# Relative-bias attention with a low-rank mixer: column halves of the first weight, an earlier cast, an even spread of the first MLP chunk, and a last output tile in two halves

## The chip, the cores and the metric

The kernel runs on one core of a Trainium2 chip. The metric is the device time of one execution in microseconds (us), as a median of several executions. The profiler's span of the same execution is some 1.8 us shorter, as it begins and ends with recorded work: 408.5 us of span belong to 410.26 us of time. A program on one core has no second die to compare with, so an execution is called fast when it lies within 1.5% of the fastest of its kernel.

## The reference, cut to what matters

```python
# q, k, v: (8 batches, 8 heads, 576 positions, 64), f32
scores = q @ k.T / 8 + bias_table[bucket(|i - j|)]         # relative-position bias
x      = softmax(scores) @ v                               # heads side by side: (8, 576, 512)
h      = (x.transpose(0, 2, 1) @ U @ V).transpose(0, 2, 1) # U, V mix positions, rank 32
u      = x + h
out    = u + relu(u @ w_ch1) @ w_ch2                       # 512 -> 2048 -> 512
```

## The kernel before

The attention runs in 32 **slots**, one for each batch and pair of heads (slots 0 to 3 are batch 0, and so on), and from slot 4 on each slot has three **segments**. The channel MLP runs in **chunks** of 512 positions: chunk 0 is batch 0, and chunk 8 takes the 64 left-over positions of all batches. A chunk has 128 matmuls of 512 columns, 64 with `w1` and 64 with `w2`. They are work that needs no VectorE or ScalarE result of the attention at hand, so they are fed into the segments one by one, to keep TensorE busy while other engines work. The generator below makes a chunk, and `Work.run(us)` issues its matmuls until so many microseconds of them are out.

```python
def chunk(j, tail):
    rhs = uT[j % 3] if j < B else uT_rem
    g = gsb.tile([128, NHT, S0], BF16, name="g")
    for nt in range(NHT):                            # 16 tiles of the hidden 2048
        gp_ = acc()                                  # one of three PSUM accumulators
        for ct in range(4):
            nc.tensor.matmul(gp_, lhsT=w1b[:, ct, nt * 128 : (nt + 1) * 128],
                             rhs=rhs[:, ct, :], start=(ct == 0), stop=(ct == 3))
            yield 0.216
        ...                                          # relu into g, by VectorE or ScalarE
    for tt in range(4):
        op = acc()
        for nt in range(NHT):
            nc.tensor.matmul(op, lhsT=g[:, nt, tt * 128 : (tt + 1) * 128],
                             rhs=w2b[:, nt, :], start=(nt == 0), stop=(nt == NHT - 1))
            yield 0.216
        ob = osb.tile([128, DM], FP32, name="ob")
        ...                                          # VectorE: ob = op + u, then the store(s)
```

Everything that turns f32 in DRAM into bf16 on chip is issued by GpSimd (POOL), in program order. The part that matters is this, with the line that issues the q and k tiles of batch 2 much later:

```python
load_w1(0)                        # w1[0:256, :]  -- rows: all columns of the first two row blocks
load_rem(1, 0); load_rem(1, 1)
qk1 = [[load_pair(which, 0) for which in range(2)]]

def more_loads():
    ...
    load_w1(1)                    # w1[256:512, :]
    ...
    for pr in range(2, NPAIR):
        qk1.append([load_pair(which, pr) for which in range(2)])
    for i in range(2):
        load_w2(i)                # 1 MB each, as bf16
# ... in the second segments of slots 4, 5, 7, 8, 9, 10: five more loads each (batch 2)
```

From slot 4 to slot 10 TensorE also transposes the q and k of the next slot. At slot 7 that is the first slot of batch 2, whose q lies in four tiles, loaded one by one:

```python
def pair_transposes(g, which):
    ...
    for t in range(NT):           # 4 tiles of q or k, and one of left-over rows
        ...
            src = qk2[which][t][:, cols]
        nc.tensor.transpose(tp[:, t * 128 : (t + 1) * 128], src, ident)
    nc.vector.tensor_copy(qkT[b % 2][:, pr, which, :], tp[:, 0:SP])
```

The softmax here doesn't subtract the row's maximum and nothing guards it: scores larger than these inputs give would overflow.

Of the kernel before, what the change touches and what calls it, by code (L numbers as in the profile page):

```python
# [15 lines left out]
ALU = mybir.AluOpType  # L16
# [14 lines left out]
def _ap_with(ap: bass.AP, offset, pattern):  # L31
    return dataclasses.replace(ap, offset=offset, ap=[list(p) for p in pattern])
# [3 lines left out]
def kernel(  # L36
# [12 lines left out]
    nc = tc.nc  # L49
    B, H, S, D = q.shape  # L50
    NB = bias_table.shape[0]
    DM = H * D
    DH = moe_w_ch1.shape[1]
# [7 lines left out]
    S0 = 512  # L61
    P4W = 704
    NPAIR = H // 2
    NHT = DH // 128
# [47 lines left out]
    w1b = const.tile([128, 4, DH], BF16)  # L112
    w2b = const.tile([128, NHT, DM], BF16)
# [225 lines left out]
    def cast_uv():  # L339
        nc.vector.tensor_copy(out=upad[:, 0:4, 0:R], in_=u_st[:, 0:4, :])  # L340
        for par in range(2):
            rows = slice(par * 64, par * 64 + 64)
            nc.vector.tensor_copy(out=upad[rows, 4 + par, 0:R], in_=u_st[rows, 4, :])
        nc.vector.tensor_copy(out=vpad[0:R, 0:S], in_=v_st)

    def load_w1(i):
        nc.gpsimd.dma_start(
            out=w1b[:, 2 * i : 2 * i + 2, :],
            in_=moe_w_ch1[i * 256 : (i + 1) * 256, :].rearrange("(t p) c -> p t c", p=128),
        )  # L350

    def load_w2(i):
# [7 lines left out]
    def acc():  # L360
        return ps_a.tile([128, 512], FP32, name="acc")
# [3 lines left out]
# [4 lines that stand above are left out]
            gp_ = acc()  # L369
            for ct in range(4):  # L370
                nc.tensor.matmul(  # L371
                    gp_,
                    lhsT=w1b[:, ct, nt * 128 : (nt + 1) * 128],
                    rhs=rhs[:, ct, :],
                    start=(ct == 0),
                    stop=(ct == 3),
                )
                yield 0.216
            if (nt % 2) if tail else clock["seg"] > 1.5:
                nc.scalar.activation(g[:, nt, :], gp_, AF.Relu)  # L380
            else:
                nc.vector.tensor_relu(out=g[:, nt, :], in_=gp_)  # L382
        for tt in range(4):
            op = acc()
            for nt in range(NHT):
                nc.tensor.matmul(  # L386
                    op,
                    lhsT=g[:, nt, tt * 128 : (tt + 1) * 128],
                    rhs=w2b[:, nt, :],
                    start=(nt == 0),  # L390
                    stop=(nt == NHT - 1),
                )
                yield 0.216
            ob = osb.tile([128, DM], FP32, name="ob")
            ur = u_tok[j % 3][:, :, tt, :] if j < B else u_rem[tt]
            nc.vector.tensor_tensor(  # L396
                out=ob.rearrange("p (a c) -> p a c", a=NPAIR),
                in0=op.rearrange("p (a c) -> p a c", a=NPAIR),
                in1=ur,
                op=ALU.add,  # L400
            )
            if j < B:
                nc.sync.dma_start(out=out[j, tt * 128 : (tt + 1) * 128, :], in_=ob)
            else:
                for par in range(2):
                    nc.sync.dma_start(
                        out=out[2 * tt + par, S0:S, :],
                        in_=ob[par * 64 : par * 64 + 64, :],
                    )

    ready = [False] * (B + 1)

    class Work:
        def __init__(self):
            self.gens = [(j, chunk(j, j >= B - 1)) for j in range(B + 1)]
            self.at = 0
            self.credit = 0.0

        def run(self, us):
            self.credit = min(self.credit + us, 4.0)  # L420
            while self.credit > 0 and self.at < len(self.gens):
                j, gen = self.gens[self.at]
                if not ready[j]:
                    self.credit = 0.0
                    return
                c = next(gen, None)
                if c is None:
                    self.at += 1
                    continue
                self.credit -= c  # L430
                clock["seg"] += c

        def finish(self):
# [132 lines left out]
    def band(g, kt):  # L566
        pr = g % NPAIR
        if kt < NKT:
            q0 = max(0, 128 * kt - 128)
            q1 = min(S, 128 * kt + 256)  # L570
            d0 = q0 - (128 * kt - 128)
            t = p_sb[g % 2][:, kt, :, q0:q1]
            e = eb[:, 2 * pr : 2 * pr + 2, d0 : d0 + q1 - q0]
        else:
            t = p4_sb[g % 2][:, 384:SP]
            e = eb4[:, pr, :]
        nc.vector.tensor_tensor(out=t, in0=t, in1=e, op=ALU.mult)  # L577
# [39 lines left out]
    def normalise(g, heads=(0, 1)):  # L617
        if g not in x_pr:
            x_pr[g] = xpp.tile([128, NT, 128], BF16, name="xp")
        xo = x_pr[g].rearrange("p t (h d) -> p t h d", h=2)  # L620
        for hh in heads:
            o = o_ps.pop((g, hh))[:, 0 : NT * 66].rearrange("p (t c) -> p t c", c=66)
            rcp = recipp.tile([128, NT], FP32, name="rcp")
            nc.vector.reciprocal(rcp, o[:, :, 64])  # L624
            rbc = _ap_with(rcp, rcp.offset, [rcp.ap[0], [1, NT], [0, 64]])
            nc.vector.tensor_tensor(  # L626
                out=xo[:, :, hh], in0=o[:, :, 0:64], in1=rbc, op=ALU.mult
            )
# [90 lines left out]
    work = Work()  # L719
# [51 lines left out]
    def emit_held(g, seg):  # L771
        now[0] = 3 * g + seg
        n = 0
        while held and (held[0][1] <= g or (held[0][0] <= now[0] and n < 2)):
            held.pop(0)[2]()
            n += 1
# [15 lines left out]
    def main_scores(g, kt):  # L792
        posts = [score(g, kt), score(g, kt + 1)]
        clock["seg"] = 0.0
        for p in posts:
            p()
# [5 lines left out]
    def rem_scores(g):  # L802
        for p in [score(g, 4), score(g, 5)]:
            p()

    def pvs(g, *ks):
        for kt in ks:
            pv(g, kt)

    def bands(g, *ks):  # L810
        for kt in ks:
            band(g, kt)
# [20 lines left out]
    kts(1, 3)  # L833
    pvs(0, 4, 0, 1, 2, 3)
    bands(1, 4, 0)
    normalise(0)
    cast_uv()
    rem_scores(2)
    kts(2, 0)
    first_transposes(3, qk0.pop(3), one)  # L840
# [45 lines left out]
    for g in range(NPAIR, NG):  # L886
        b, pr = divmod(g, NPAIR)
        for seg in range(3):
            emit_held(g, seg)
            box = []  # L890
            if seg:
                main_scores(g, 2 * seg - 2)
            else:
                box = remainder_scores(g)
            if seg == 1:
                n = 0
                if g == NPAIR or g == 2 * NPAIR or (pr == 3 and 1 < b < B - 2):
                    pool_order += load_tasks(b + 1 if pr == 0 else b + 2)
                if g in (4, 5, 7, 8, 9, 10):
                    n = 5  # L900
                elif b > 1:
                    if pr == 3 and b < B - 2 or pr in (0, 2) and b < B - 1:
                        n = 5
                if n:
                    nc.gpsimd.tensor_copy(out=gate, in_=x_pr[g - 1][0:1, 0, 0:2])  # L905
                    for _ in range(n):
                        pool_order.pop(0)()
            work.run(1.7 if g < 2 * NPAIR + 2 else 2.2)
            for p in box:
                p()  # L910
            if g == NPAIR:
                pass
            elif seg == 0:
                if g > NPAIR + 1:
                    mix_h(g - 2)
            elif seg == 2:
                mix_t(g - 1, nc.scalar.copy)
            if seg and NPAIR < g < 2 * NPAIR:
                put_off.pop(0)()
            if seg == 0:  # L920
                if g + 1 < 3 * NPAIR:
                    pair_transposes(g + 1, 0)
                band(g, 4)
                if g > NPAIR:
                    pv_head(g - 1, 0)
            elif seg == 1:
                if g + 1 < 3 * NPAIR:
                    pair_transposes(g + 1, 1)
                band(g, 0)
                band(g, 1)  # L930
                if g > NPAIR:
                    pv_head(g - 1, 1)
                if b > 1 and pr == 1:
                    ready[b - 1] = True
            else:
                band(g, 2)
                band(g, 3)
    assert not pool_order and not held
    g = NG - 1
# [48 lines left out]
```

## Time and profile before

| kernel before | |
|---|---|
| time, median (lowest to highest) | 410.66 us (410.39 to 410.82) |
| span of the profiled execution | 408.5 us |
| TensorE busy | 389.5 us, 95% |
| full stretch of TensorE | 96 to 403.7 us |

The prediction below goes through the page and the timelines. One more view of the kernel before turned out to be the most useful, and I made it only afterwards: the busy time in three stretches that are cut at events of TensorE itself. The columns are the window, its length, the busy time of PE (TensorE), PEld (its weight loads), DVE (VectorE), ACT (ScalarE) and POOL with counts, then granted clock, DMA share and GB/s.

```profile
36.60:39.03 2.43, 1.71 (x16) 0.85 (x14) 0.92 (x3) 1.45 (x3) 1.23 (x2) 1.00 2.18 148
39.03:94.06 55.03, 53.20 (x582) 30.84 (x579) 42.54 (x96) 29.58 (x39) 30.50 (x44) 1.00 1.39 130
94.06:408.50 314.44, 309.26 (x2735) 164.45 (x2733) 173.34 (x367) 147.98 (x207) 67.80 (x96) 1.00 0.76 87
```

I call what lies ahead of the first window **stage A** (start to the first MLP matmul), and the three windows **B** (to the first matmul of slot 4), **C** (to the first matmul of chunk 1) and **D** (to the end). What to see: B, C and D are lengths between two events in one execution, so a late start does not enter them, except where a transfer's landing decides. These views end at the span as the page prints it, rounded to 0.1 us. For D, where differences of 0.07 us matter, the text and the table take the end from the trace's last record (408.49 us here, so D is 314.43).

### The profile page before, as it was taken

To read this page: it belongs to the slowest core of one execution; us is meant where nothing else is said; L and a number is where in the kernel's file an instruction comes from. 1 tells how busy PE (TensorE), PEld (TensorE's weight loads), DVE (VectorE), ACT (ScalarE), POOL (GpSimd) and SP (SyncE) were. 2 spreads that over 40 slices of the span, in tenths; PEclk is the share of its full clock that TensorE was granted. 3 is DMA by queue.
4 is the path that set the end of the run, shared out by engine and by line. 5 is a ranking of instruction groups with operands and counts; after the bars stand their busy time and mean duration, and the time that the engine had idled before them with its cause. 6 is when DMAs were issued, how large, how long until landed. Compare 5 with 4: busy or idle time off the path is not lost.

```text
span 408.5 us, 9084 instructions
## 1 busy us (share of the span) xinstructions
PE 389.5 (95%) x3684; PEld 212.8 (52%) x3684; DVE 246.3 (60%) x558; ACT 205.0 (50%) x284; POOL 125.7 (31%) x179
## 2 busy tenths in 40 slices
PE   3779999999999999999999999999999999999995
PEld 1456555555555555555555555555555554444442
DVE  6886897667765667557754785567656732422421
ACT  5877555556655565556555655556555530220310
POOL 3968924454454045404540454040000000000000
PEclk9799999999999999999999999999999999999999
DMA  7999999999999699949996999399022003001013
GB/s 129 170 170 161 114 189 120 118 118 116 174 69 128 131 117 86 129 104 150 92 102 132 128 89 106 94 138 96 14 66 66 14 14 104 26 14 73 18 27 77
DMA packets 162082, 40.68 MB, mean 100 GB/s; under 512 B 151760, under 2 KB 156888, under 8 KB 162040
## 3 DMA queue, kind: packets, MB, share of 16 engines
q0 software_dynamic: 107904, 17.97, 61.2%
q1 hardware_dynamic: 53320, 21.74, 26.2%
q8 instruction: 29, 0.48, 0.5%
q10 hardware_dynamic: 816, 0.39, 0.4%
q14 instruction: 13, 0.11, 0.1%
HBM read 37.84 MB, written 9.45 MB: 116 GB/s over the span
## 4 chain that ended last, share of the span: by engine, by line
PE 82%; DMA 8%; POOL 6%; DVE 2%; issue 1%; ACT 1%; ACTq 0%; DVEq 0%; POOLq 0%
PE acc L386 31%; PE acc L371 28%; PE o L601 10%; PE sc L514 7%; DMA w1b<-in_moe_w_ch_dram 4%; DMA qb<-in_k_dram 3%; PE acc L637 2%; POOL qb L265 2%; POOL v_bf L255 2%; PE acc L653 1%; PE sc L527 1%; PE sc L548 1%; DMA gp_dram<-gp 1%; DVE ob L396 1%; POOL eb L213 1%
## 5 line engine op out<-in xcount | busy, mean ns | idle before, releaser
L523 ACT ACTIVATE p_sb<-sc 128x1024 bf16<-128x1024 f32 x128 | 124.4, 1022 | 100.4 <-PE sc L514 100.3
L386 PE MATMUL acc<-w2b,g 128*128 128x512 bf16 x576 | 132.4, 379 | 0.0
L371 PE MATMUL acc<-uT,w1b 128*128 128x512 bf16 x512 | 119.5, 380 | 0.6 <-DMA w1b<-in_moe_w_ch_dram 0.4
L371 PEld LDWEIGHTS <-w1b 128*128 128x128 bf16 x576 | 53.2, 98 | 72.4 <-issue 13.1
L386 PEld LDWEIGHTS <-g 128*128 128x128 bf16 x576 | 53.6, 98 | 70.6 <-issue 10.6
L382 DVE TENSOR_SCALAR g<-acc 128x512 bf16<-128x512 f32 x95 | 65.3, 690 | 34.4 <-PE acc L371 33.1
L577 DVE TENSOR_TENSOR p_sb<-p_sb,eb 128x768 bf16<-128x768 bf16 (+3 forms) x160 | 71.3, 472 | 10.0 <-ACT p_sb L523 9.4
L601 PEld LDWEIGHTS <-p_sb 128*128 128x128 bf16 x1600 | 56.1, 98 | 9.2 <-DVE p_sb L577 1.6
L601 PE MATMUL o<-v_bf,p_sb 128*128 128x65 bf16 x1500 | 58.0, 194 | 2.3 <-DVE xp L626 0.9
L380 ACT ACTIVATE g<-acc 128x512 bf16<-128x512 f32 x49 | 29.3, 598 | 59.8 <-PE acc L371 44.5
L396 DVE TENSOR_TENSOR ob<-acc,u_tok 128x512 f32<-128x512 f32 x32 | 22.1, 691 | 49.9 <-PE acc L386 49.9
L514 PE MATMUL sc<-qkT 64*128 64x512 bf16 x256 | 41.3, 392 | 1.5 <-ACT qkT L459 0.7
L905 POOL COPY gate<-xp 1x2 bf16<-1x2 bf16 x18 | 3.5, 197 | 121.5 <-DVE xp L626 121.5
L661 DVE TENSOR_TENSOR u_tok<-acc,xp 128x512 bf16<-128x512 f32 x32 | 22.1, 691 | 23.9 <-PE acc L653 23.7
L626 DVE TENSOR_TENSOR xp<-o,rcp 128x320 bf16<-128x320 f32 x60 | 29.5, 492 | 3.2
L255 POOL DMA_DIRECT2D v_bf<-in_v_dram x32 | 28.4, 911 | 1.7 <-DMA w1b<-in_moe_w_ch_dram 1.4
L255 POOL DMA_DIRECT2D qb<-in_k_dram x24 | 21.7, 906 | 5.8 <-DMA w2b<-in_moe_w_ch_dram 4.2
L255 POOL DMA_DIRECT2D qb<-in_q_dram x24 | 21.9, 913 | 4.7 <-DVE g L382 4.7
L557 ACT ACTIVATE p_sb<-sc 128x640 bf16<-128x640 f32 x32 | 22.3, 698 | 0.2
L540 ACT ACTIVATE p_sb<-sc 128x512 bf16<-128x512 f32 x32 | 19.1, 598 | 5.6 <-PE sc L527 3.9
L624 DVE RECIPROCAL rcp<-o 128x5 f32<-128x5 f32 x60 | 11.5, 191 | 13.7 <-PE o L601 13.2
L645 ACT CAST tt<-acc 128x128 bf16<-128x128 f32 x32 | 8.6, 267 | 14.3 <-PE acc L637 13.8
(90 smaller groups left out, 260.8 us busy)
## 6 DMA issues: line engine op xcount, KB each, us to landing
out_dram<-ob SPq DMA_DIRECT2D x32, 256.0 KB, 2.4
v_bf<-in_v_dram POOLq DMA_DIRECT2D x32, 128.0 KB, 5.9
qb<-in_q_dram POOLq DMA_DIRECT2D x27, 128.0 KB, 4.9
qb<-in_k_dram POOLq DMA_DIRECT2D x27, 128.0 KB, 4.9
w1b<-in_moe_w_ch_dram POOLq DMA_DIRECT2D x2, 1024.0 KB, 8.7
w2b<-in_moe_w_ch_dram POOLq DMA_DIRECT2D x2, 1024.0 KB, 12.6
out_dram<-ob SPq DMA_DIRECT2D x8, 128.0 KB, 2.4
stage<-gp_dram SPq DMA_DIRECT2D x4, 192.0 KB, 4.7
```

Of the source, the lines that this page charges most:

```text
L255: nc.gpsimd.dma_start(out=dst, in_=src[b, :, t * 128 : (t + 1) * 128, :].rearrange("h p d -> p h d"),)
L371: nc.tensor.matmul(gp_, lhsT=w1b[:, ct, nt * 128 : (nt + 1) * 128], rhs=rhs[:, ct, :], start=(ct == 0), stop=(ct == 3),)
L380: nc.scalar.activation(g[:, nt, :], gp_, AF.Relu)
L382: nc.vector.tensor_relu(out=g[:, nt, :], in_=gp_)
L386: nc.tensor.matmul(op, lhsT=g[:, nt, tt * 128 : (tt + 1) * 128], rhs=w2b[:, nt, :], start=(nt == 0), stop=(nt == NHT - 1),)
L396: nc.vector.tensor_tensor(out=ob.rearrange("p (a c) -> p a c", a=NPAIR), in0=op.rearrange("p (a c) -> p a c", a=NPAIR), in1=ur, op=ALU.add,)
L514: nc.tensor.matmul(sp[:, hh, :], lhsT=kT[rows, i * 128 : (i + 1) * 128], rhs=qT[rows, 0:S0], start=True, stop=True,)
L523: nc.scalar.activation(P[:, i, :, 0:S0], sp, AF.Exp, scale=scale)
L557: nc.scalar.activation(P4[:, 0:SP], sp.rearrange("p a c -> p (a c)")[:, 0:SP], AF.Exp, scale=scale,)
L577: nc.vector.tensor_tensor(out=t, in0=t, in1=e, op=ALU.mult)
L601: nc.tensor.matmul(o[:, qt * 66 : qt * 66 + 65], lhsT=lhs[:, c0 : c0 + 128], rhs=rhs, start=(kt == NKT and qt == 0), stop=(kt == NKT - 1), ...
L626: nc.vector.tensor_tensor(out=xo[:, :, hh], in0=o[:, :, 0:64], in1=rbc, op=ALU.mult)
```

## The change

The intent was to fill TensorE's idle time before 96 us and to shorten the end. Chunk 0 needs all rows of `w1`'s first columns, so it is loaded by column halves. The cast of the mixing weights U and V moves into an idle moment of VectorE. Chunk 0's 128 matmuls are spread evenly over 17 segments rather than 8 to a segment until they run out. The last tile's add and store start with half of its columns, and the final stores use two queues.

```diff
     def load_w1(i):
+        cols = slice(i * DH // 2, (i + 1) * DH // 2)
         nc.gpsimd.dma_start(
-            out=w1b[:, 2 * i : 2 * i + 2, :],
-            in_=moe_w_ch1[i * 256 : (i + 1) * 256, :].rearrange("(t p) c -> p t c", p=128),
+            out=w1b[:, :, cols],
+            in_=moe_w_ch1[:, cols].rearrange("(t p) c -> p t c", p=128),
         )
 ...
+            pieces = (0, 256, 512) if j == B and tt == 3 else (0, 512)
+            for c0, c1 in zip(pieces, pieces[1:]):
+                w = c1 - c0
+                for nt in range(NHT):
+                    nc.tensor.matmul(
+                        op[:, c0:c1],
+                        lhsT=g[:, nt, tt * 128 : (tt + 1) * 128],
+                        rhs=w2b[:, nt, c0:c1],
 ...
+                    yield 0.216 * w / 512
 ...                                  # the add of columns c0:c1
+                    for par in range(2):
+                        (nc.scalar if par else nc.sync).dma_start(
+                            out=out[2 * tt + par, S0:S, c0:c1],
+                            in_=ob[par * 64 : par * 64 + 64, c0:c1],
+                        )
 ...
+        def even(self, segs):
+            self.run(0.216 * (NHT * 8 - self.done) / segs)
 ...
     bands(1, 4, 0)
+    cast_uv()
     normalise(0)
-    cast_uv()
 ...
-            work.run(1.7 if g < 2 * NPAIR + 2 else 2.2)
+            if 3 * g + seg < 6 * NPAIR + 5:
+                work.even(6 * NPAIR + 5 - 3 * g - seg)
+            else:
+                work.run(2.2)
```

More of the change, by code (lines that the diff above doesn't have):

```diff
@@ L384, in chunk @@
             op = acc()
-            for nt in range(NHT):
-                nc.tensor.matmul(
-                    op,
-                    lhsT=g[:, nt, tt * 128 : (tt + 1) * 128],
-                    rhs=w2b[:, nt, :],
-                    start=(nt == 0),
-                    stop=(nt == NHT - 1),
-                )
-                yield 0.216
             ob = osb.tile([128, DM], FP32, name="ob")
             ur = u_tok[j % 3][:, :, tt, :] if j < B else u_rem[tt]
-            nc.vector.tensor_tensor(
-                out=ob.rearrange("p (a c) -> p a c", a=NPAIR),
-                in0=op.rearrange("p (a c) -> p a c", a=NPAIR),
-                in1=ur,
-                op=ALU.add,
-            )
-            if j < B:
-                nc.sync.dma_start(out=out[j, tt * 128 : (tt + 1) * 128, :], in_=ob)
-            else:
-                for par in range(2):
-                    nc.sync.dma_start(
-                        out=out[2 * tt + par, S0:S, :],
-                        in_=ob[par * 64 : par * 64 + 64, :],
-                    )
+            pieces = (0, 256, 512) if j == B and tt == 3 else (0, 512)
[6 more added lines that the diff above has]
+                        rhs=w2b[:, nt, c0:c1],
+                        start=(nt == 0),
+                        stop=(nt == NHT - 1),
+                        skip_group_check=True,
+                    )
+                    yield 0.216 * w / 512
+                nc.vector.tensor_tensor(
+                    out=ob[:, c0:c1].rearrange("p (a c) -> p a c", c=128),
+                    in0=op[:, c0:c1].rearrange("p (a c) -> p a c", c=128),
+                    in1=ur[:, c0 // 128 : c1 // 128, :],
+                    op=ALU.add,
+                )
+                if j < B:
+                    nc.sync.dma_start(out=out[j, tt * 128 : (tt + 1) * 128, :], in_=ob)
+                else:
[3 more added lines that the diff above has]
+                            in_=ob[par * 64 : par * 64 + 64, c0:c1],
+                        )
     ready = [False] * (B + 1)
@@ L417, in __init__ @@
             self.credit = 0.0
+            self.done = 0
+        def even(self, segs):
+            self.run(0.216 * (NHT * 8 - self.done) / segs)
         def run(self, us):
@@ L430, in run @@
                 self.credit -= c
+                self.done += 1
                 clock["seg"] += c
@@ L907 @@
                         pool_order.pop(0)()
-            work.run(1.7 if g < 2 * NPAIR + 2 else 2.2)
+            if 3 * g + seg < 6 * NPAIR + 5:
+                work.even(6 * NPAIR + 5 - 3 * g - seg)
+            else:
+                work.run(2.2)
             for p in box:
```

## The prediction

> **What bounds the kernel now.** I began with the page: the share of each engine, then the chain that ended last.
>
> ```profile
> span 408.5 us, 9084 instructions
> ...
> PE 389.5 (95%) x3684; PEld 212.8 (52%) x3684; DVE 246.3 (60%) x558; ACT 205.0 (50%) x284; POOL 125.7 (31%) x179
> ...
> PE 82%; DMA 8%; POOL 6%; DVE 2%; issue 1%; ACT 1%; ACTq 0%; DVEq 0%; POOLq 0%
> ```
>
> TensorE is the bound; DMA and POOL stand in the chain only near the start. The busy time by window says where TensorE is not full (columns: window, length, then PE, PEld, DVE, ACT, POOL busy with counts, clock, DMA share, GB/s). The windows are the start, slots 1 to 3, 4 to 6, 7 to 9, the rest of the attention in two parts, the pure matmul tail, and the end.
>
> ```profile
> 0.00:20.00 20.00, 11.37 (x104) 6.24 (x105) 15.56 (x60) 13.67 (x18) 13.81 (x24) 0.87 1.07 148
> 20.00:39.03 19.03, 15.64 (x269) 11.29 (x269) 14.86 (x37) 13.76 (x21) 13.55 (x19) 0.96 1.33 169
> 39.03:67.71 28.68, 27.99 (x278) 15.64 (x276) 24.00 (x50) 15.49 (x20) 19.18 (x26) 1.00 1.73 148
> 67.71:96.07 28.36, 27.21 (x319) 16.27 (x317) 19.85 (x48) 15.98 (x21) 13.33 (x20) 1.00 1.04 111
> 96.07:200.00 103.93, 103.93 (x1050) 57.61 (x1048) 67.64 (x150) 60.57 (x84) 40.09 (x58) 1.00 1.25 120
> 200.00:330.00 130.00, 129.65 (x1304) 71.86 (x1303) 83.05 (x183) 73.00 (x101) 25.70 (x36) 1.00 0.72 86
> 330.00:403.70 73.70, 73.67 (x371) 33.92 (x369) 20.65 (x32) 12.53 (x22) 0.00 (x0) 1.00 0.14 43
> 403.70:408.50 4.80, 0.00 (x0) 0.00 (x0) 0.69 (x1) 0.00 (x0) 0.00 (x0) 0.86 0.24 55
> ```
>
> From 96 us to 403.7 us TensorE is full at clock 1.00, and the diff removes no matmul column, so only the first 96 us and the last 4.8 us can give anything. The timeline of each engine shows the particular waits (start, length, operation, idle before).
>
> ```profile
> 22.75 0.40 DVE L340 CAST upad<-u_st 128x128 bf16<-128x128 f32 x1
> ...
> 37.56 0.39 PE L371 MATMUL acc<-uT,w1b 128*128 128x512 bf16 x1 [0.36 <-DMA w1b<-in_moe_w_ch_dram]
> ...
> 70.50 0.38 PE L488 MATMUL acc<-ident,qb 128*128 128x128 bf16 x4
> ...
> 91.49 0.22 PE L488 MATMUL acc<-ident,rem 128*128 128x128 bf16 x1
> 92.66 0.93 PE L601 MATMUL o<-v_bf,p_sb 128*128 128x65 bf16 x25 [0.95 <-DVE xp L626]
> ...
> 62.70 0.88 POOL L255 DMA_DIRECT2D qb<-in_k_dram  x1 [4.20 <-DMA w2b<-in_moe_w_ch_dram]
> ...
> 65.30 0.90 POOL L255 DMA_DIRECT2D qb<-in_q_dram  x1
> ...
> qb<-in_q_dram POOLq DMA_DIRECT2D x1, 128.0 KB, 4.8
> ```
>
> Each is one of the waits that the change aims at, or runs into. The last line is the DMA view for the window 65.2 to 65.4: issue to landing.
>
> **What the Trainium skill says.** "PSUM — Partial Sum Buffer", section "PSUM bank collisions raise a hardware error": TensorE writing and VectorE reading one bank and quadrant at once is an error even at disjoint columns. Half the last output tile lies in the same bank as the other half. The trace before cannot show this; the built program can, and does (below). "TensorE: Matmul & The Clock Gate", "Back-to-back issue gap", gives N/2.4 + 2.5 ns for an isolated matmul, about 216 ns at 512 columns, but also a sustained 131 ns. The chain's 13.81 us for 64 such matmuls, 216 ns, sides with the first. "DMA: Bandwidth & Descriptors", Specifications, puts line rate at 512 B and over. The packets of w1 go from 4 KB to 2 KB, so no rate should be lost; the packet records agree, as w1 in 4 KB packets (1 MB from 20.8 us to its landing at 27.6 us) and w2 in 1 KB packets (2 MB in 48.0 to 61.5 us) move at about 154 and 155 GB/s.
>
> **The change part by part.**
>
> w1 by column halves. Chunk 0's first tile needs all four row blocks of w1's first columns; before, two of them come with the second load, which lands at 37.51 (issued 29.40, 8.11 us). With column halves all that is needed lands with the first load, at 27.61. The wait of 0.36 us goes. Behind it the next matmuls wait for xp, whose last VectorE operation ends at 37.56, so they move only from 37.78 to about 37.6: some 0.15 us. The second half is needed near 49 us, so it is hidden.
>
> Casts. They hold VectorE from 22.75 to 24.05, 1.30 us; the two transposition copies behind them start at 24.05 but could start when their transposes end, at about 23.6. Before, VectorE also idles 1.20 us ahead of 21.48, where the casts now go. So the copies come 0.43 us earlier, and with them the matmuls at 25.83 and ScalarE's row from 26.67 to 35.86, which is nearly without gaps. Both parts together: slot 4 starts about 0.55 us earlier.
>
> Even spread. Before, a segment holds 8 chunk matmuls (1.73 us) until chunk 0 runs out, and slot 9's second segment has none: TensorE stands from 91.54 to 92.66, 1.1 us, for VectorE. The new order has 7 or 8 in each of 17 segments, seven of them there: 1.51 us of work covers the wait. Two waits for an accumulator still with VectorE, 0.29 us before 70.50 and 0.24 us before 77.88, also become shorter. Against this the tile boundaries fall elsewhere; the order of the new program, each accumulator set against the evacuation that frees it, suggests about 0.2 us of new small waits. So slots 7 to 9 give 1.31 + 0.29 - 0.2, about 1.4 us, if nothing else holds them.
>
> Last tile in halves. Sixteen matmuls of 256 columns take 1.73 us. VectorE takes 0.69 us for 512 columns and 0.28 us for 128 (its L704 rows), so by the line through both 0.42 us for 256. In the new program the first matmul of half two waits for the very VectorE add that reads half one (I matched the semaphore's value to the instruction). TensorE thus stops for about 0.17 us of matmul latency (a modelled 0.39 us less the 0.216 us pitch), 0.42 us and a handover of 0.05 us: 0.65 us. The last add then ends at 403.71 + 0.65 + 0.42 = 404.78, against 404.40: 0.4 us later. The two final stores go out in parallel on two queues instead of one after the other, which saves one issue of 0.56 us, and each is half as large: perhaps 0.1 us. Net -0.25 us.
>
> **The rivals.** (a) *A transfer takes the place of the removed waits; I hold this for the likeliest.* The transposes at 70.50 (slot 7, first segment) need all four q tiles of batch 2. The fourth is issued at 65.30 and lands 4.8 us later, at 70.1, only 0.4 us before use. Its issue hangs on w2's second load (62.70 waits for it), which hangs on POOL's issues and the DMA queue, not on TensorE. In the new kernel TensorE arrives there 0.55 us earlier from the start and six chunk matmuls (77 done instead of 83, 1.30 us) earlier from the spread, so at about 68.3; it waits near 1.9 us. Then it leaves at about 70.2 with 1.30 us of chunk work still owed: 0.3 - 1.30 + 1.31 - 0.2 = 0.1 us gained by slot 9's end. If the w1 halves land 0.2 us later each, as twice the packets may cost, POOL and w2 come later too, and 0.1 gained becomes 0.3 lost. Both start parts buy only a longer wait. (b) *Nothing holds it:* 0.55 + 1.4 + 0.25 = 2.2 us gained, 408.4. For it: before, the gap at 70.50 ended with VectorE, not DMA. Against it: the 0.4 us of slack. (c) *VectorE becomes the bound in slots 4 to 6:* it is busy 24.00 of 28.68 us, and with fewer matmuls per segment TensorE meets its evacuations sooner. That would raise small waits there by perhaps 0.5 us, but under (a) these are swallowed by the wait for q: no effect on the time; under (b) 408.9.
>
> **Range and chances.** (a) with -0.1 to +0.3 us before the tail and -0.25 us there gives 410.3 to 410.7; (b) 408.4. Weighted some three to one for (a), and with a small start gain that the arithmetic may have missed, 410.2. The lower end is (b), 408.3; the upper adds 1 us of w1 landing later to (a), 411.6. Two per cent is 8.2 us, more than all idle time of TensorE after 20 us that the change touches, so "same" is all but certain.
>
> **What would show it right or wrong.** In the new profile: no wait for w1 near 37 us; the casts before 21.6; slot 4 about 0.5 us earlier; a TensorE wait of 1.5 to 2.5 us for qb before the first transposes of slot 7, with the fourth q tile landing at 70.0 to 71.0; no wait near 91; and a TensorE stop of about 0.65 us between the halves of the last tile, with the last store issued from two engines. The prediction is wrong if w2 lands earlier (then q does, and (b) holds), if w1's halves take over 1 us more, or if TensorE has new waits after 96 us, where the tile boundaries move as well.

## The result, and the profile after

The changed kernel takes 409.35 us in the median of four executions (408.93 to 410.12), beside 410.52 us (410.19 to 410.82) for the kernel before on the same chip. The ratio is 0.9974, with a 95% interval of 0.9956 to 0.9991: some 1.1 us faster, far below two per cent. A ratio here is the mean time of one kernel's fast executions over the mean of the other's in the same rounds, so it is not quite the ratio of the two medians. The time lies inside the predicted range, but 0.85 us below the predicted 410.2.

The page and the three stages of the changed kernel:

```profile
span 407.1 us, 9061 instructions
...
PE 386.2 (95%) x3636; PEld 214.7 (53%) x3700; DVE 245.5 (60%) x558; ACT 205.7 (51%) x285; POOL 125.1 (31%) x179
```

```profile
36.17:38.47 2.30, 1.70 (x17) 0.84 (x15) 0.92 (x3) 1.45 (x3) 0.81 (x1) 1.00 2.02 157
38.47:92.99 54.52, 52.24 (x571) 30.82 (x579) 41.01 (x92) 30.17 (x40) 31.79 (x46) 1.00 1.44 130
92.99:407.10 314.11, 306.62 (x2699) 166.05 (x2749) 174.15 (x371) 147.97 (x207) 66.58 (x94) 1.00 0.74 88
```

First a warning about the page. There are 3700 weight loads but 3636 matmuls: 64 matmul records are missing from this trace. TensorE's busy time of 386.2 us is too small for that reason, and idle time in which a group is one short and "issue" is named (0.16 us, several times) is no idle time. Stage lengths don't suffer from it. They say: stage A 0.43 us shorter (36.60 to 36.17), B 0.13, C 0.51 and, to the traces' last records, D 0.29 (314.43 to 314.14), together the 1.4 us between the two spans.

Now TensorE's timeline of the changed kernel (start, length, engine, line, operation, out and in, shapes, count, and in brackets the idle time before it with what ended it):

```profile
37.00 0.38 PE L372 MATMUL acc<-uT,w1b 128*128 128x512 bf16 x1 [0.24 <-ACT uT L704]
...
68.92 0.33 PE L498 MATMUL acc<-ident,qb 128*128 128x128 bf16 x3
69.77 0.23 PE L498 MATMUL acc<-ident,qb 128*128 128x128 bf16 x1 [0.52 <-DMA qb<-in_q_dram]
...
91.55 0.22 PE L498 MATMUL acc<-ident,rem 128*128 128x128 bf16 x1
91.61 0.91 PE L611 MATMUL o<-v_bf,p_sb 128*128 128x65 bf16 x25
...
401.42 1.91 PE L392 MATMUL acc<-w2b,g 128*128 128x256 bf16 x16 [0.52 <-DVE ob L401]
```

What to see, line by line against the kernel before: the matmul that waited for `w1` now waits for ScalarE's `uT` (37.00). At slot 7 three of four transposes run at once and only the fourth waits for its q tile. It starts 0.85 us after the three, of which some 0.17 us are their own issue, so TensorE stands for 0.68 us (the 0.52 in the bracket counts from a modelled end). The gap of 1.1 us near 91.5 is gone. And the second half of the last tile waits for the add that reads the first half.

VectorE's and then GpSimd's timeline of the changed kernel:

```profile
20.18 0.31 DVE L340 CAST upad<-u_st 128x128 bf16<-128x128 f32 x1
...
400.95 0.42 DVE L401 TENSOR_TENSOR ob<-acc,u_rem 128x256 f32<-128x256 f32 x1 [1.05 <-PE acc L392]
403.37 0.43 DVE L401 TENSOR_TENSOR ob<-acc,u_rem 128x256 f32<-128x256 f32 x1 [2.00 <-PE acc L392]
```

```profile
61.76 0.88 POOL L255 DMA_DIRECT2D qb<-in_k_dram  x1 [3.51 <-DMA w2b<-in_moe_w_ch_dram]
...
64.36 0.90 POOL L255 DMA_DIRECT2D qb<-in_q_dram  x1
```

The casts start at 20.18 instead of 22.75. The add of 256 columns takes the predicted 0.42 us. The issue of batch 2's fourth q tile still hangs on `w2` (61.76 waits for it) and comes at 64.36; by the DMA view it lands 5.37 us later, at 69.73. The fourth transpose starts at 69.77.

Why a q or k tile waits for `w2` at all, the traces show: GpSimd's loads signal their landing on eight semaphores (completion counters) in turn. In the fourteen traces 2002 loads have a recorded landing eight places before them, and none of them is issued before that landing; for seven places, 120 of 2016 are. So a load waits for the eighth load before it. At 61.76 that is the second half of `w2`; the loads behind it follow in program order. Whether the chip or the built program asks for this is not shown.

### The profile page after: what moved, and what is told of

It is laid out like the page before. It is cut to its first block, busy times and chain, and to the rows that moved or that the text cites. A ratio compares the mean times of both kernels' runs of the same rounds, so it can differ in the third digit from the quotient of the medians.

```text
span 407.1 us, 9061 instructions
## 1 busy us (share of the span) xinstructions
PE 386.2 (95%) x3636; PEld 214.7 (53%) x3700; DVE 245.5 (60%) x558; ACT 205.7 (51%) x285; POOL 125.1 (31%) x179
## 4 chain that ended last, share of the span: by engine, by line
PE 81%; DMA 11%; POOL 5%; issue 2%; DVE 1%; ACT 0%; DVEq 0%; POOLq 0%
PE acc L392 30%; PE acc L372 27%; PE o L611 10%; PE sc L524 7%; DMA w1b<-in_moe_w_ch_dram 4%; DMA w2b<-in_moe_w_ch_dram 3%; PE acc L647 2%; POOL v_bf L255 2%; PE acc L663 1%; POOL qb L265 1%; DMA qb<-in_q_dram 1%; PE sc L537 1%; PE sc L558 1%; DMA tblT<-in_bias_table_dram 1%; DMA gp_dram<-gp 1%
## 5 line engine op out<-in xcount | busy, mean ns | idle before, releaser
L392 PE MATMUL acc<-w2b,g 128*128 128x512 bf16 (+1 forms) x560 | 128.6, 373 | 2.3 <-DVE ob L401 0.5
L372 PE MATMUL acc<-uT,w1b 128*128 128x512 bf16 x484 | 116.3, 380 | 2.5 <-issue 0.6
L392 PEld LDWEIGHTS <-g 128*128 128x128 bf16 x592 | 55.1, 98 | 70.2 <-issue 11.7
L587 DVE TENSOR_TENSOR p_sb<-p_sb,eb 128x768 bf16<-128x768 bf16 (+3 forms) x160 | 71.1, 473 | 10.1 <-ACT p_sb L533 9.5
L647 PEld LDWEIGHTS <-upad 128*128 128x128 bf16 x160 | 11.4, 98 | 7.7 <-DVE xp L636 0.7
```

Source lines behind the costliest of these rows:

```text
L392: nc.tensor.matmul(op[:, c0:c1], lhsT=g[:, nt, tt * 128 : (tt + 1) * 128], rhs=w2b[:, nt, c0:c1], start=(nt == 0), stop=(nt == NHT - 1), s ...
L587: nc.vector.tensor_tensor(out=t, in0=t, in1=e, op=ALU.mult)
```

## The experiments

There were twelve runs in three calls. Each call has its own chip and its own executions of the kernel before (medians 410.65, 410.29 and 410.41 us, 11 each), and every ratio is against those. The main theory was that the q tile at slot 7 gives back part of what the change gains. The rivals were that the start parts are worthless in themselves, and that the loss lies in the tail's stop.

All stages first. Each row is the profiled execution of one kernel. The bold words say which parts it has.

| kernel | A | B | C | D | span | ratio (95%) |
|---|---|---|---|---|---|---|
| before | 36.60 | 2.43 | 55.03 | 314.43 | 408.5 | 1 |
| **tail** only | 36.69 | 3.28 | 55.01 | 314.13 | 409.1 | 0.9995 (0.9984 to 1.0006) |
| **start** only | 36.02 | 2.29 | 55.16 | 314.43 | 407.9 | 0.9993 (0.9980 to 1.0006) |
| **spread** only | 36.98 | 2.93 | 53.82 | 314.44 | 408.2 | 0.9973 (0.9959 to 0.9987) |
| **all** (the change) | 36.17 | 2.30 | 54.52 | 314.14 | 407.1 | 0.9974 (0.9956 to 0.9991) |
| all, again | 36.42 | 2.30 | 55.18 | 314.13 | 408.0 | 0.9974 (0.9957 to 0.9990) |
| all, **without start** | 36.89 | 2.93 | 53.84 | 314.12 | 407.8 | 0.9982 (0.9969 to 0.9996) |
| all, second accumulator | 35.85 | 2.30 | 54.89 | 313.45 | 406.5 | 0.9970 (0.9959 to 0.9982) |
| all, last tile whole | 36.83 | 2.30 | 54.20 | 314.20 | 407.5 | 0.9970 (0.9958 to 0.9981) |
| all, w2 half later | 36.80 | 2.30 | 55.29 | 314.14 | 408.5 | 1.0058 (1.0033 to 1.0083) |
| all, w2 half earlier | 36.28 | 2.30 | 53.83 | 314.13 | 406.5 | 0.9955 (0.9940 to 0.9969) |
| w2 earlier, without start | 36.50 | 2.90 | 53.84 | 314.13 | 407.4 | 0.9960 (0.9945 to 0.9975) |
| w2 earlier, second accumulator | 37.91 | 2.30 | 53.84 | 313.47 | 407.5 | 0.9929 (0.9913 to 0.9945) |
| the same, again | 36.17 | 2.30 | 53.91 | 313.45 | 405.8 | 0.9935 (0.9923 to 0.9947) |

Read down a column. **B** is 2.29 or 2.30 in all nine traces with `w1` by column halves, and 2.43 to 3.28 with row halves. **C** is 55.0 to 55.2 without the spread. With it, C is 53.82 to 53.84 in five traces and longer in the other six, by the wait for q: in all eleven TensorE takes 30.45 to 30.47 us from slot 4's start to the first transposes of slot 7 and 23.20 to 23.22 us from the fourth transpose to chunk 1, and only the time between these two varies. **D** has four values: 314.43 or 314.44 without the tail part, 314.20 with two queues, 314.12 to 314.14 with halves as well, 313.45 to 313.47 with a second accumulator. The runs of "start" have the column halves and the early casts together; no run has one without the other. **A** is between 35.85 and 37.91, and no part of the change orders it. One execution's span is therefore no measure of a gain of half a microsecond; a stage is.

### Call 1: is it the tail, the start, or the transfer?

**A second accumulator for the second half**, so that it doesn't share a bank of PSUM (the memory that TensorE writes its sums to) with the half that VectorE reads:

```diff
             for c0, c1 in zip(pieces, pieces[1:]):
                 w = c1 - c0
+                if c0:
+                    op = acc()
```

> The changed kernel, but the second half of the last output tile accumulates in a PSUM buffer of its own. My theory: the stop of TensorE between the two halves (0.68 us in the changed kernel's trace) comes from sharing one bank with the half that VectorE reads, so it goes, the last add ends 0.6 to 0.7 us earlier after the last full tile, and the time falls by about 0.65 us. Rival: the stop is the cost of starting a new group of narrow matmuls; then it stays, and the time is the same as the changed kernel's.

Measured: 409.45 us (408.30 to 409.99). VectorE's timeline of it shows the two adds:

```profile
401.00 0.42 DVE L403 TENSOR_TENSOR ob<-acc,u_rem 128x256 f32<-128x256 f32 x1 [1.05 <-PE acc L394]
402.74 0.42 DVE L403 TENSOR_TENSOR ob<-acc,u_rem 128x256 f32<-128x256 f32 x1 [1.32 <-PE acc L394]
```

The adds are 1.74 us apart, the time of 16 half matmuls, rather than 2.42 as in the changed kernel. The stop of 0.68 us is gone, and D is 0.69 us shorter. So it is shown that the stop comes from writing the buffer that VectorE still reads, and not from starting a new group of matmuls. Since a new buffer is also a new bank, the run doesn't tell which of the two the program guards. In the times of this call the gain doesn't show: the ratio is that of the changed kernel. In call 2 it does, as told below.

**The last tile whole, on two queues:** `pieces = (0, 512)`.

> The changed kernel, but the last output tile in one piece again; its two stores still go out from two engines. My theory: the split as written costs more than it gives (stop 0.68, plus a last add of 0.43 instead of 0.69: the last add ends 0.42 us later than for a whole tile), and all that the new ending gains comes from the second store queue. So this is 0.2 to 0.4 us faster than the changed kernel, from the end of the last full tile to the end of the span. Rival: halving the last add and stores is the gain; then this is 0.2 to 0.6 us slower.

Measured: 409.33 us (409.12 to 409.49); D is 314.20. The expectation that the whole tile would be 0.2 to 0.4 us better than the halves missed: D is level with that of the halves (0.07 us longer), and so is the time. But the run splits the sum of the tail into its terms, since it has the second queue alone. The second queue saves 314.43 - 314.20 = 0.23 us. What the halves add to it is a stop of 0.68 us (2.42 - 1.74), and they save 314.20 - 313.45 = 0.75 us by a shorter last add and smaller stores.

**All without the start parts:** `w1` by row halves, the cast after the first normalisation, the rest as changed.

> The changed kernel without its two early parts: w1 in row halves, casts behind the normalisation. My theory: slot 4 starts 0.5 to 0.6 us later, but the transposes at slot 7 wait for the fourth q tile of batch 2 (0.68 us in the changed kernel's trace), so the wait there shrinks to about 0.1 us and the work after it stands where it stood, within 0.15 us: same time. Rival: the early gain passes through; then everything from slot 7 on is 0.55 us later.

Measured: 409.88 us (408.77 to 410.91). C is 53.84, so there is no wait for q at all. Slot 4 began late, at 39.82, and TensorE came to the transposes at 70.28, just after the tile had landed. What the start parts take from B they give back in C, here at least: B 2.93 against 2.30, C 53.84 against 54.52. The ratio, 0.9982, is not told apart from the changed kernel's 0.9974.

**The second half of w2 after batch 2's first q and k tiles**, meant to free the q tile:

```diff
-        for i in range(2):
-            load_w2(i)
+        load_w2(0)
 ...
                     for _ in range(n):
                         pool_order.pop(0)()
+                    if g == NPAIR:
+                        load_w2(1)
```

> The changed kernel, but w2's second half is issued behind the first three q and k tiles of batch 2 instead of in front of them, so that the fourth q tile no longer waits for it. My theory: that tile lands at 66 to 67 us, before TensorE comes for it at 68.9; the wait of 0.68 us goes and the time falls by 0.5 to 0.7 us, unless w2's second half now lands later than its first use at about 67.6 us, which would show as a new wait for w2b. Rival: the wait for the q tile only stands in for another (an accumulator or an exponential), and the time stays.

Measured: 412.94 us (410.33 to 414.30), slower than the kernel before, against every expectation. GpSimd's and TensorE's timelines of it:

```profile
46.39 0.97 POOL L354 DMA_DIRECT2D w2b<-in_moe_w_ch_dram  x1
...
47.76 1.26 POOL L282 DMA_DIRECT2D rem<-in_q_dram  x2
48.99 1.25 POOL L282 DMA_DIRECT2D rem<-in_k_dram  x2
50.20 0.94 POOL L255 DMA_DIRECT2D qb<-in_q_dram  x1
51.08 0.93 POOL L255 DMA_DIRECT2D qb<-in_k_dram  x1
51.96 0.94 POOL L255 DMA_DIRECT2D qb<-in_q_dram  x1
57.27 0.88 POOL L354 DMA_DIRECT2D w2b<-in_moe_w_ch_dram  x1 [4.38 <-DMA w2b<-in_moe_w_ch_dram]
```

```profile
71.17 0.23 PE L498 MATMUL acc<-ident,qb 128*128 128x128 bf16 x1 [1.02 <-DMA qb<-in_q_dram]
```

The second half had become the eighth load after the first (four loads of left-over rows and three of q and k lie between), so GpSimd had to wait for the first half's landing before it could issue the second. Just after that the DMA queues moved only 66 GB/s (from 58 to 60 us, against 202 in the changed kernel). The fourth q tile was issued at 61.01, over 3 us earlier, but took 10.1 us to land rather than 5.4. The edit moved the wait and made it longer. Between 410.3 and 414.3 us its executions spread more than any other kernel's. Why some of them are 3 us slower than the profiled one I have not found; no slow execution was profiled.

### Call 2: remove the wait for q by loading earlier instead

**The changed kernel again**, as a control, with a second profile:

> The changed kernel itself, for the same chip and the same rounds as the three beside it: a ratio of 0.997 within 0.001, slot 4 at 38 to 39.2 us according to how fast the start runs, and whatever that is, the fourth transpose of slot 7 at 69.7 to 70.2 us.

Measured: 409.53 us (408.47 to 409.84), ratio 0.9974 as before. TensorE's timeline of this execution, at slot 7:

```profile
69.18 0.33 PE L498 MATMUL acc<-ident,qb 128*128 128x128 bf16 x3
70.68 0.23 PE L498 MATMUL acc<-ident,qb 128*128 128x128 bf16 x1 [1.17 <-DMA qb<-in_q_dram]
```

The same kernel waits 1.33 us here (1.50 less the 0.17 of issue), against 0.68 in the first profile, because the tile landed at 70.64. In four executions with the changed kernel's loads and the spread, C exceeds 53.83 by 0.37, 0.69, 1.06 and 1.35 us, on average 0.87. The spread itself is worth 55.03 - 53.83 = 1.20 us.

**The first half of w2 two loads earlier**, between the third and the fourth head pair of batch 1:

```diff
-        for pr in range(2, NPAIR):
-            qk1.append([load_pair(which, pr) for which in range(2)])
         for i in range(2):
+            qk1.append([load_pair(which, 2 + i) for which in range(2)])
             load_w2(i)
```

> The changed kernel, but the first half of w2 is issued before the last pair of batch 1's q and k tiles, some 3 us earlier, into a stretch (38 to 47 us) where the DMA rate was only 70 to 150 GB/s. My theory: w2's second half lands near 60 instead of 61.5 us, the fourth q tile of batch 2 at about 67.5, before TensorE comes for it at 68.9: the wait of 0.6 us goes, and slot 9's third segment starts 0.6 us earlier relative to slot 4. Rival: the DMA queue is limited by POOL's issues or by bytes that only move around; then the tile still lands near 69.7 and nothing is gained.

Measured: 408.47 us (408.27 to 409.09). GpSimd's and TensorE's timelines of it:

```profile
60.45 0.88 POOL L255 DMA_DIRECT2D qb<-in_k_dram  x1 [2.51 <-DMA w2b<-in_moe_w_ch_dram]
```

```profile
69.04 0.39 PE L498 MATMUL acc<-ident,qb 128*128 128x128 bf16 x4
```

GpSimd's wait for `w2` ends 1.3 us earlier than in the changed kernel, the fourth q tile lands 5.14 us after 63.05, at 68.19, and all four transposes run together at 69.04. C falls to 53.83, its shortest value. The two medians of this call differ by 1.06 us, near the 0.87 us of mean wait, and the ratio goes from 0.9974 to 0.9955. The intervals overlap (0.9957 to 0.9990 and 0.9940 to 0.9969), but time and trace agree. The wait for q is what the changed kernel gives back: that is shown in the traces, and in the times it is only likely.

**The same without the start parts:**

> The same without the two early parts (w1 in row halves, casts behind the normalisation). My theory: with the wait for the q tile gone, the early parts are worth their full 0.5 to 0.6 us, so this is slower than the kernel beside it by that much, where with the wait in place leaving them out cost less. Rival: the early parts are worth nothing, or the same with and without the wait.

Measured: 408.86 us (408.22 to 409.16), 0.4 us above the version with the start parts. B says that the start parts are worth 0.6 us there on the mean of five row-half executions (2.43, 2.90, 2.93, 2.93, 3.28; mean 2.89, against 2.30). The times are in agreement with that, but don't resolve it.

**w2 earlier and a second accumulator together:**

> w2 early and the last tile's second half in a bank of its own. If both theories hold, the two gains add: 0.6 us at slot 7 and 0.65 us at the end, about 1.2 us faster than the changed kernel, near 408.2 us. If the stop at the end or the wait at slot 7 only stands in for something else, one of them is missing.

Measured: 407.60 us in the median (406.93 to 409.29), ratio 0.9929. This is the best version, so I let it run once more in call 3. Against w2 earlier alone it is 0.9 us faster, where the trace of call 1 promised 0.68; the two intervals overlap a little (0.9940 to 0.9969 and 0.9913 to 0.9945).

### Call 3: each part alone

**Start only** (column halves and the early cast on the kernel before):

> The kernel before plus only the first two parts (w1 by column halves, casts ahead of the first normalisation). Theory (q wait): slot 4 starts about 0.55 us earlier (near 38.5), and the first transposes of slot 7 would be reached near 69.9 with 82 chunk matmuls done; the fourth q tile lands near 69.7 to 70.1, so TensorE waits 0 to 0.3 us for it; the gap of about 1 us near 91 stays. Time 0.3 to 0.5 us below the kernel before, ratio 0.9988 to 0.9993. Rival (the start parts are worthless): ratio 1.000 and slot 4 at the old place. Rival (the start parts alone carry the whole gain): ratio 0.997.

Measured: 409.99 us (409.39 to 410.93). The stage view and TensorE's timeline of it:

```profile
38.31:93.47 55.16, 53.33 (x581) 30.85 (x579) 42.51 (x96) 29.57 (x39) 30.69 (x45) 1.00 1.44 131
```

```profile
92.08 0.93 PE L602 MATMUL o<-v_bf,p_sb 128*128 128x65 bf16 x25 [0.95 <-DVE xp L627]
```

As expected, the gap near 91 stays (0.95 us), the wait for q takes little (C is 0.13 us longer than before; the tile landed at 70.03, the transposes began at 69.78), and slot 4 starts at 38.31. The gain of 0.3 us in the ratio is not told apart from none by its interval, though it is the expected size.

**Spread only:**

> The kernel before plus only the even spread of chunk 0. Theory: slot 4 at the old 39.0, slot 7's transposes reached near 69.5 (five matmuls fewer done), the fourth q tile (landing near 70.1) makes TensorE wait about 0.3 us, the gap near 91 goes, and chunk 1 starts about 0.7 us earlier than before (93.3 instead of 94.06). Time 0.6 to 0.9 us below the kernel before, ratio 0.9978 to 0.9985. Rival (the q wait takes all that the spread gives, my prediction's likeliest case): ratio 0.9995 to 1.000.

Measured: 409.44 us (408.47 to 409.95), ratio 0.9973. Its stage view and, from TensorE's timeline, the wait for `w1` that it keeps:

```profile
39.91:93.73 53.82, 53.01 (x581) 30.83 (x579) 40.80 (x92) 30.17 (x40) 31.30 (x45) 1.00 1.41 131
```

```profile
38.43 0.39 PE L371 MATMUL acc<-uT,w1b 128*128 128x512 bf16 x1 [0.86 <-DMA w1b<-in_moe_w_ch_dram]
```

This one part has the gain of the whole change: 0.9973 against 0.9974. I had expected 0.6 to 0.9 us and a wait for q of 0.3 us; it gives 1.1 us and has no wait. The reason stands in its second line. Row halves let `w1` come late, slot 4 starts at 39.91, and TensorE comes to the transposes at 70.36, after the tile (issued at 65.53, landed at 70.27). A late start hides the q tile, and an early one exposes it.

**Tail only:**

> The kernel before plus only the last tile in two halves with its stores on two queues. Theory (from the trace of the changed kernel): span from the unstalled end of TensorE's work 4.45 us instead of 4.80, so 0.35 us below the kernel before, ratio 0.9991; a stop of 0.65 to 0.70 us between the halves. Rival: the stop eats all, ratio 1.000. If front, spread and tail alone sum to the whole (about 1.1 us), the parts are independent; if front and spread alone sum to more than the two together, the q wait absorbs the difference.

Measured: 410.23 us (409.48 to 410.91). Two lines of it, from TensorE's timeline and from the stages:

```profile
38.49 0.39 PE L371 MATMUL acc<-uT,w1b 128*128 128x512 bf16 x1 [1.21 <-DMA w1b<-in_moe_w_ch_dram]
```

```profile
94.98:409.10 314.12, 309.46 (x2751) 166.05 (x2749) 173.34 (x368) 147.96 (x207) 67.71 (x96) 1.00 0.75 87
```

D is 0.31 us shorter than before, as it is, by 0.29 to 0.31, in every kernel with halves and one accumulator. This run also shows why a span misleads: its own is 0.6 us *longer* than that of the kernel before, because `w1` landed late in that execution (1.21 us of wait, and B 3.28). Its median is 0.2 us shorter.

By ratio, start, spread and tail alone give 0.7, 2.7 and 0.5 thousandths, 3.9 in sum or 1.6 us. Together they give 2.6, or 1.1 us. The difference of 0.5 us is of the size and sign of the wait for q. With intervals of 1.1 to 1.4 thousandths on each it is not proved by the times alone.

**The best version again:**

> The changed kernel with the first half of w2 issued two loads earlier and with an accumulator of its own for the second half of the last tile, once more, with a second profile: no wait for q at slot 7, no stop between the halves, 407.3 to 408.2 us, ratio 0.993 to 0.995. If the first result (0.9929) was luck, it comes back at the 0.9955 of the version without the second accumulator.

Measured: 407.76 us (407.17 to 408.25), ratio 0.9935. It beats the kernel before by 2.7 us and the changed kernel by some 1.6 us, as the difference of ratios (0.9974 and 0.9935, of different calls) has it. C is 53.91 and D 313.45, so both hold. The race for the q tile is close even here: the tile landed at 69.11 and TensorE began the transposes at 68.92, which cost 0.07 us.

## Why the prediction was right or wrong

**The sum.** The measured 409.35 us lies between the cases (a) and (b); neither came true whole. The prediction's own weighting doesn't give its 410.2: three parts of 410.5, the middle of (a), and one of 408.4 make 410.0, and a further start gain would lower that. So some 0.2 of the 0.85 us are a slip of the sum.

**The bound was right.** D is the same in all fourteen traces up to the differences in the last tile, so after chunk 1 starts nothing but the tail can be gained, as said.

**w1 by column halves: right in kind, too small in size.** The wait for `w1` went, and the second half of `w1` was hidden (it landed at 37.38). The prediction put the part at 0.15 us. In the two traces compared it is 0.13 us. But the profile before had caught a lucky execution: with row halves B is 2.43 there and 2.90 to 3.28 in the four others. The mean worth is 0.6 us. This counts all of B's gain as the column halves', because the wait for `w1` is what is gone from it (0.36 us in the profile before, 0.83 to 1.21 in the other four); no run without the early casts checks that. The term failed because it rested on one execution of a transfer's landing.

**The casts: the same order, and not measurable.** Their place was as said, the copies behind them came 0.46 us earlier (24.05 to 23.59, predicted 0.43), and stage A of the two traces differs by 0.43 us. Over all traces the mean of A is 36.73 us with late casts and 36.49 with early ones, but A wanders by 2 us, so the runs neither confirm nor deny 0.4 us. What makes A wander is open.

**The even spread: near.** Predicted 1.4 us, less 0.5 for rival (c)'s small waits in slots 4 to 6 if nothing hides them, so 0.9. Measured in C, without a wait for q: 1.20 us. From slot 4's start to the first transposes TensorE takes 31.47 us before and 30.45 with the spread, with five chunk matmuls (1.08 us) fewer. So its waits there grew by 0.06 us in sum: the 0.29 us before 70.50 went, and others grew by some 0.35.

**The wait for q: the mechanism was right, and its size failed.** Rival (a) was called likeliest: the transposes of slot 7 would wait for the fourth q tile, 1.9 us, and net 0.1 us would remain of start and spread. The wait is there, but in none of the four traces as long as the 1.5 us that the prediction asked for: it is 0.35 to 1.33 us. TensorE came at 68.92 in the first trace, not at 68.3, since one matmul fewer was moved (0.22 us) and the small waits of slots 4 to 6, which the prediction took as swallowed, came before the transposes (0.35). In the first trace the net gain up to chunk 1 is not 0.1 but 1.07 us. The terms, each by what it measured:

- The tile landed at 69.73, not near 70.1: 0.37 us.
- Only the fourth transpose needs it. I had all four start after the landing, where three are done by then, and I rounded the start up to 70.2: 0.22 us together.
- Five chunk matmuls are moved behind the transposes, not six: 82 were done there before, and I had counted 83, as one earlier segment holds seven. That makes 1.08 us owed and not 1.30: 0.22 us.
- From the fourth transpose to chunk 1 TensorE took 23.39 us before and 23.22 after, with 1.08 us more of chunk work, so 1.25 us of waits were saved there against the 1.31 - 0.2 = 1.11 predicted: 0.14 us.

These sum to 0.95, and 0.1 + 0.95 = 1.05 us. In the second trace of the same kernel the tile landed at 70.64. Its C is 55.18, longer than the 55.03 of before, and its chunk 1 starts at 93.90, only 0.16 us earlier than before. That execution is close to the predicted case. So the failed step is to have given this wait one length. It is a race between a transfer (landing from 69.7 to 70.6) and TensorE's arrival (the first transposes at 68.6 to 69.6 in the four traces), and it costs 0.4 to 1.4 us, 0.87 on average.

**"Both start parts buy only a longer wait": largely so.** They gain 0.6 us in B, and the kernels without them have no wait for q. The spread alone is as fast as the whole. This was the prediction's idea, but it had the wait eat the spread's gain too, which it does not on average.

**Column halves didn't slow the loads.** The prediction feared 0.2 us later landings. From its issue, GpSimd's release by the first `w1` load came after 9.49 to 10.86 us with row halves (five traces) and 9.90 to 10.58 with column halves (nine). If anything the queue behind it moved up: the fourth q tile was issued at 65.30 to 65.55 in the four row-half traces with `w2` in its old place, and at 64.25 to 64.92 in the five such with column halves. It then took 5.2 to 5.7 us to land instead of 4.7 or 4.8, so it was hardly there sooner (69.7 to 70.6 us against 70.1 to 70.3).

**The tail: the net was near by two errors that cancel.** That is luck. Predicted -0.25, measured -0.30 us. The stop was predicted as 0.65 and is 0.68, for the cause given, and the half-width add is 0.42 as said. But a second queue saves 0.23 us, not a whole issue of 0.56. The halves save 0.75 us, of which the add is 0.69 - 0.42 = 0.27. So the half-size stores are worth some 0.48 (the last store lands 2.22 us after the last add rather than 2.62, which says 0.40), not 0.1.

**Left open:** why w2 later has executions of 414 us; why the second accumulator, 0.66 to 0.69 us of D in all three of its traces, shows in the times only together with the earlier `w2`; and what moves stage A.

## What to carry to other kernels

Before making an early stage faster, list what the next stages take from queues that don't get faster with it. If a transfer lands 0.4 us before it is needed, only the first 0.4 us of an earlier arrival is kept, and the rest turns into waiting. Here reordering the loads (the first half of `w2` earlier) was worth 0.8 us by the ratios, where the whole change was worth 1.1. And count the loads: here each one waited for the eighth before it, so one large load held up a small one that has nothing to do with it. Half-microsecond effects are measured between two events of one execution, over several executions, not on spans: here an unrelated start moved by 2 us, and one profile showed a wait of 0.36 us that others showed as 0.83 to 1.21. If a tile's second half is to run while the first is read, give it another accumulator; here that took away the whole stop of 0.68 us.

## What the Trainium skill lacked or had wrong

- "TensorE: Matmul & The Clock Gate", section "Back-to-back issue gap": the sustained 131 ns for 512 columns doesn't appear here. The final chunks keep 216 ns for each matmul (13.81 us for 64), which the same section gives as the isolated gap.
- "DMA: Bandwidth & Descriptors", section "Anatomy of one DMA — SWDGE (gpsimd) path": the fit of 2.0 us plus bytes over 436 GB/s would give 6.8 us for the 2 MB of f32 that a `w1` load reads, or 4.4 us for the 1 MB of bf16 that it writes (estimates from the page). The 28 such loads of the fourteen traces took 7.95 to 10.57 us from issue to landing, in a queue with smaller loads, and 2 MB of `w2` as bf16 came from 48.0 to 61.5 us, or 155 GB/s. The page has no rate for converting loads, and no run here has one alone in the queue.
- The same page, section "Rules for kernel authors", says that spreading DMAs over issuing engines only saves sequencer issue time. That agrees in kind: a second queue for two final stores saved 0.23 us. On one queue the second store is issued 0.51 us after the first, on two 0.01 us after; but the store that ScalarE issued took 2.59 us to land, where SyncE's second had taken 2.38 in the kernel before. The page doesn't tell of that difference, and one trace each is little to go by.
- No page says how GpSimd's loads hold each other up. Here their landings are told by eight semaphores in turn, and none of 2002 loads was issued before the one eight places ahead had landed; an issue waited 4.38 us for a 1 MB load with seven smaller ones issued in between. This may be the built program's doing and not the chip's. Putting one such load later made the q tile behind it take 10.1 us to land and not 5.4.
